# Attention rows of tiles 10 to 31 transposed by 32x32 blocks and DMA, with a new order of instructions

## Chip, cores, metric

One Trainium2 chip, one of its cores. The metric is the device time of one execution in microseconds (us); the kernel before is given as the median of three runs.

## The reference

Two blocks, applied twice in turn to one sequence of 2048 rows of 512 (bf16): attention with a sliding window of 256 and 32 heads of 16, and an MLP with 1792 hidden units.

```python
def _A_ref(x, wqkv, wo):
    B, S, D = x.shape
    H = 32; Dh = D // H; W = 256
    qkv = (x @ wqkv).reshape(B, S, 3, H, Dh)  ...
    scores = jnp.einsum("bhqd,bhkd->bhqk", q, k) * (Dh ** -0.5)
    mask = (idx[:, None] - idx[None, :] >= 0) & (idx[:, None] - idx[None, :] < W)
    p = _softmax(jnp.where(mask[None, None], scores, -1e9), axis=-1)
    o = jnp.einsum("bhqk,bhkd->bhqd", p, v)
    return o.transpose(0, 2, 1, 3).reshape(B, S, D) @ wo

def _B_ref(x, w1, b1, w2, b2):
    return jnp.einsum("bsf,fd->bsd", _gelu(x @ w1 + b1), w2) + b2

x = A_x
for _ in range(2):
    x = x + _A_ref(_layernorm(x), A_wqkv, A_wo)
    x = x + _B_ref(_layernorm(x), B_w1, B_b1, B_w2, B_b2)
```

## The kernel before

The rows are cut into 16 tiles of 128, and because the two blocks are applied twice the kernel counts tiles (tau) from 0 to 31; tile tau works on the rows of tau modulo 16. Attention goes by blocks of two tiles, b = 0 to 15. X holds all rows in SBUF and is updated in place.

For each tile and each of the two layers (0 is attention, 1 is the MLP) `layernorm` takes the statistics on VectorE (DVE), a power on GpSimd (POOL), and writes the normalised rows, xn, on DVE. The projections need these rows transposed. This is done in one of two ways:

- On TensorE (PE): four 128x128 transposes into a PSUM bank (the function `tr`, line 36 of the profile, since a helper records every PE operation as line 32 or 36), then a copy out by DVE (line 916) or ScalarE (ACT, line 918).
- By blocks and DMA, where `by_dma` says so; in the kernel before for the MLP rows of tiles 4 to 29. DVE transposes each 32x32 block in place of its own (line 952) into xs_, four DMAs write it to a scratch array scr_x in DRAM in pieces of 256 bytes (line 956), and one DMA reads it back into xnTB in pieces of 1024 bytes (line 960). All DMAs are issued by SP, in order, and xs_ has three buffers.

xnTB, the MLP's input, keeps the four 32-row groups of a tile outside the four feature chunks, so a partition's row is one piece of 1024 bytes. xnTA, the input of the Q, K and V projections, has the chunk outside and the 256 rows of a block contiguous, as both operands of PE read it. xnTA has two halves, so block b+2 can be written only when PE has finished Q, K and V of block b. The V projections of a block are late in PE's order, the Q projections of the next are the first to need the new contents.

Attention of a block: groups of scores (32x64 tiles of PE, 64 to 320 columns) into pairs of PSUM banks, exponentials on ScalarE (line 1111), mask products on DVE or POOL (line 1132), the product with V on PE into a pair of banks, a stream transpose of the result on DVE (line 1197), reciprocal and product (1200, 1202), a transpose back (1207), the output projection and the residual (990). An MLP job takes two or four tiles: W1 matmuls, Gelu on ScalarE (1269, 1278), W2 matmuls, residual.

Nothing is scheduled on the chip. `_Plan` holds a node for each piece of work, with its engine, a planned duration, what it reads and writes, and for PE the class of PSUM banks it needs. ORDER, a list of node numbers written out in the file, sets the order on every engine; a negative number takes a node's alternative engine. `_Plan.follow` walks it and gives each PSUM request the candidate in its pool that comes free first. `_Sched` turns the nodes into instructions with semaphore waits. SP's DMAs take turns on 12 semaphores, and a DMA waits for the one that had the semaphore before it.

Of the kernel before, what the change touches and what calls it, by code (L numbers as in the profile page):

```python
# [6 lines left out]
dt = mybir.dt  # L7
# [511 lines left out]
def bass_interleave_layers__sliding_block__dense_activation_gelu__prompt_kernel(  # L519
# [42 lines left out]
    NXS = 3  # L562
    NSC = 16

    def by_dma(tau, layer):
        return layer and 4 <= tau < NT - 2
# [23 lines left out]
    def mm(n):  # L590
        return n / 2.4 + 2.6

    with ExitStack() as kctx:
        S_ = _Sched(nc, kctx)

        def sb(name, shape, dtype=dt.bfloat16):
# [21 lines left out]
        scr = nc.dram_tensor("scr_x", (NSC, 4, 32, 4, P), dt.bfloat16, kind="Internal").ap()  # L618
# [17 lines left out]
            0, 18, 1, 19, 2, 20, 8, 4, 5, 21, 6, 14, 7, 22, 15, 16, 9, 23, 33, 10, 24, 11, 40, 12, 34, 3, 41, 17, 35,  # L636
            42, 84, 36, 43, 85, 86, 37, 44, 38, 77, 87, 45, -40, 88, -47, 78, 89, 79, 80, 47, 57, 58, 81, 59, 60, 90,
            82, 61, 52, -84, 48, 49, 50, 91, -52, 92, 229, 25, 93, 94, 53, 26, 108, -96, 54, 55, 96, 109, -57, 101,
            154, 62, 155, 63, 102, 230, 64, 103, 236, 65, 72, 156, 67, 110, 66, 68, 111, 69, 70, -72, 145, 112, 73,
            231, 104, 146, 358, 74, 75, 232, 97, 98, 359, 76, 147, 99, 135, 136, 237, 105, 158, 28, -101, 815, 137, 27,  # L640
            160, 138, 360, 106, 139, 361, 113, 29, 140, 141, 159, 13, 30, 107, 142, 143, 365, -149, 149, -145, 114,
            125, 366, 126, 587, -163, 115, 31, 127, 32, 128, 594, 151, 150, 116, 117, 118, 588, 233, 163, -120, 595,
            129, -162, 120, 165, 121, 122, 253, 123, 951, -154, 254, 164, 183, 367, 958, 255, 256, 184, 368, 238, 124,
            -153, 257, 185, 187, 130, 131, 239, 240, 188, 132, 816, 234, 133, 596, 189, 235, 597, 178, 134, 241, -167,
            180, 263, 258, 259, 242, 264, 179, 369, 192, 362, 265, 959, 193, 266, 960, 589, 191, 243, 248, 167, 249,
            194, 244, 182, 245, 190, 246, 250, 822, 251, -268, 168, 157, -253, 186, 268, 169, 260, 961, 247, 261, -196,
            262, 170, 172, 173, -197, 174, 286, 269, 287, 270, -182, 271, 363, 817, 175, 288, 364, 273, 171, 370, 272,
            274, -177, 197, 371, 198, 275, 291, 199, 293, -277, 372, 373, 200, 292, 177, 277, 374, 823, 375, 279, 290,
            378, 376, 379, -202, 278, 377, 282, 295, 283, 384, 281, 385, 380, 202, -295, 381, 284, 311, 382, 386, 387,
            313, 289, 216, 217, 388, 218, -281, 203, -384, 219, 204, 312, 205, 220, 206, -286, 315, 207, 316, 208, 300,  # L650
            317, 209, 296, 210, 221, 211, 301, 298, 222, 212, 223, 302, 297, 224, 320, 322, 225, 213, 214, 226, -300,
            321, 227, 404, 430, 405, -320, 431, 416, 432, 417, 420, 406, 418, 421, 306, 323, 325, 413, 307, 414, 422,
            -319, 427, 415, 423, 428, 308, 424, 429, 408, 824, 425, 459, 410, 464, 310, 465, 444, 469, 309, 466, 467,
            460, 598, 409, 445, 446, 470, 303, 389, 314, 390, 391, 304, 392, 326, 590, 305, 215, 439, 447, 468, 393,
            440, 441, 442, 433, 449, 327, 443, 952, 419, 450, 328, 451, 434, 426, 471, 452, 472, 454, 461, 453, 462,
            455, 435, 473, 436, 591, 437, 456, 448, 457, 329, 518, 438, 411, 399, 463, -331, 400, 458, 401, 402, 592,
            403, 489, 394, 228, 395, 331, 396, 397, 520, 490, 398, 491, 492, 493, 593, 519, 494, 412, 504, 332, -408,
            505, 333, 334, 335, 495, 336, 506, 496, 508, 497, 337, 498, 510, -508, 345, 346, 338, 347, 348, 509, 513,
            349, -522, 499, 500, 515, 501, 502, 474, -512, 503, 475, 514, 476, 533, 1216, 599, 825, 535, 477, 600, 478,
            479, 339, 516, 480, 534, 481, 350, 340, 528, 482, 517, 530, 483, 512, 484, 485, 351, 486, 352, 341, 529,  # L660
            487, 953, 353, 342, 488, 537, 354, 539, 522, 343, -533, 1209, 355, 538, 523, 356, 357, 542, 524, 671, 543,
            672, -532, 657, 658, 673, 544, 640, 525, 324, 664, 1210, 665, 641, 1211, 659, 668, -546, 669, 666, 654,
            655, 642, 670, 644, 656, -537, 661, 662, 646, 601, 663, 602, 603, 541, 604, 645, 606, 540, 635, 1217, 546,
            607, 636, 526, 608, 547, 527, -649, 637, 609, 548, 610, -606, -640, 649, 549, 611, 650, 616, 617, -644,
            618, 619, 651, 550, 612, 620, 631, 818, 613, 632, 614, -552, 705, 675, 676, 615, 706, 677, 707, 708, 690,
            678, 685, 344, 686, 691, 680, 552, 692, 687, 681, 688, 693, 660, 682, 683, 570, 652, 571, 694, 647, 572,
            689, 573, 653, 553, 667, 826, 554, 555, 819, 709, 556, 574, 710, 674, 711, 712, 713, 695, 696, 557, 679,
            697, 698, 700, 684, 701, 702, 575, 703, 621, 699, 622, 714, 558, 623, 624, 704, 626, 627, 559, 625, 628,
            629, 715, 576, 630, 716, 717, 820, 633, 577, 764, 821, 718, 560, 766, 827, 561, 719, 828, 720, 578, 721,
            765, 829, 634, 830, 831, 638, 755, 579, 749, 757, 580, 962, 750, 756, 832, -834, 759, 770, 751, 722, 771,  # L670
            723, 724, 725, 726, 772, 562, 745, 563, 834, 747, 835, 773, 567, 836, 1218, 774, 837, 565, 727, 746, 838,
            728, 583, 760, 566, 729, 730, 762, 581, 731, 748, 732, 564, 733, 758, 734, 761, 769, 863, 752, 735, 736,
            865, 763, 737, 738, 767, 739, 1345, 568, 864, 775, 584, 753, 582, 776, 754, -868, 877, 777, 849, 878, 850,
            740, 741, 742, 879, 778, 743, 868, -780, 744, 851, 869, 852, 839, 853, 840, -882, 841, 870, 842, 780, 859,
            844, 843, 860, 845, -872, 846, 847, 861, 848, 901, -769, 854, 855, 902, 856, 862, 857, 781, 954, 858, 782,
            903, 872, 955, 783, 1219, 784, 874, 798, 785, 799, -867, 800, 801, 873, 786, 892, 956, 802, 894, 963, -876,
            975, 957, 976, 787, 977, 964, 893, 978, 788, 803, 897, 789, 965, 899, 966, 804, 876, 880, 898, 805, 790,
            882, 806, 791, 967, 884, 886, 807, 794, 808, 814, 792, 883, 968, 795, 887, 1346, 979, 810, -970, 793, 811,
            905, 1004, 812, 888, 970, 1006, 809, 585, 1005, 1352, 796, 995, 896, 980, 981, 997, 885, 982, 983, 900,
            813, 996, -905, 906, 971, 984, 972, 908, 973, 1212, -896, 907, 974, 1008, 1043, 1009, 909, 1044, 910, 1045,  # L680
            1010, 911, 889, 999, -891, 1046, 1000, 1047, 1050, -1013, 891, 1001, 1060, 1347, 1048, 1061, -999, 912,
            1062, -1004, 1033, 913, 985, 1034, 1051, 569, 986, 987, 1052, 1035, 988, 1018, 989, 990, 1020, 991, 914,
            992, 993, 915, 1053, 1019, 994, 1013, 1054, 1014, 916, -1022, 1233, 1234, 1055, 1235, 1015, 1236, 1028,
            1007, 917, 1237, 1030, 918, 919, 920, 1074, 934, 1029, 921, 1075, 1076, 1077, 1017, 1038, 1213, 1057, 1032,
            1039, 1353, 1058, 1031, 1011, 935, 1040, 1089, 1016, 1090, 1064, 1354, 1002, 1065, 922, 1066, 1022, 1059,
            1067, 923, 1049, 1023, 1094, 1024, 1068, 1095, 1079, 1080, 1078, 1081, 1082, 924, 1091, 1083, 1092, 925,
            1069, 1099, 1093, 926, 1100, 1101, 1355, 1070, 1063, 1071, -1037, 1096, 936, 937, 1056, 586, 1072, 938,
            1102, 1097, 1084, 1103, 1085, 939, 933, 1086, 1087, 1073, 1266, 940, 941, 927, 1104, 1098, 797, 1105, 1106,
            1088, 1107, 929, 1108, 1109, 928, 1110, 942, 1111, 1112, 943, 1113, 1114, 944, 1149, -1042, 1267, 1214,
            1150, 1215, 1151, 947, 1152, 1025, 1268, 1115, 945, 1026, 1253, 948, 1153, 1255, 1220, 1154, 930, 1155,  # L690
            1037, 946, 1116, 1117, 1254, 1156, 1118, 1257, 1157, 1258, 1158, 1590, 1159, 1160, 1027, 1161, 949, 1162,
# [176 lines left out]
        for h in range(NZ):  # L868
            PL.root = (add("pe", clear, 8 * mm(512), reads=["zero", "g0"], writes=["ps:init0", "ps:init1"], prio=-200, geo="f"),)
# [489 lines left out]
```

## Time and profile before

| | |
|---|---|
| median of three runs | 462.32 us (461.71 to 462.74) |
| profiled execution: its time, its span | 461.4 us, 459.7 us |
| PE busy | 442.2 us, 96%, 8793 matmuls |
| DVE busy | 370.0 us, 81% |
| ACT busy | 394.2 us, 86% |
| POOL busy | 216.5 us, 47% |
| PE transposes | 152 (38 tiles), of these 128 for attention |
| granted TensorE clock | 1.00 |
| DMA, all queues | 27855 packets, 18.17 MB |
| scr_x writes | 104, 32 KB each, 1.6 us to landing |
| xnTB reads | 26, 128 KB each, 2.1 us to landing |

An engine's busy share is over the whole span; the busy tenths show it in 40 slices. The chain of waits follows the work that ended last back to its releaser at every step, so it tells which engine sets the time in each stretch. Idle time in front of a group is given with what ended it. PE's busy time is modelled where matmuls overlap.

### The profile page before, as it was taken

How to read it: one execution, taken by the hardware profiler on the slowest of the kernel's cores; microseconds unless marked ns; L12 is line 12 of the kernel's file. 1: busy time of each engine (PE TensorE's matmuls, PEld its weight loads, DVE VectorE, ACT ScalarE, POOL GpSimd, SP SyncE). 2: the span in 40 equal slices, each digit the busy share in tenths (PEclk: the TensorE clock that was granted, in tenths of full speed). 3: DMA queues.
4: the chain of work that ended last, by engine and by line, in shares of the span. 5: the costliest groups of instructions: out<-in, count | busy, mean ns of one | idle time of the engine just before them, and what ended most of it. 6: DMA issues, size and time to landing. Idle time of an engine off the chain costs nothing.

```text
span 459.7 us, 19399 instructions
## 1 busy us (share of the span) xinstructions
PE 442.2 (96%) x8793; PEld 236.5 (51%) x8793; DVE 370.0 (81%) x754; ACT 394.2 (86%) x473; POOL 216.5 (47%) x250
## 2 busy tenths in 40 slices
PE   6987899999889999999999999999999999999997
PEld 3654465754444445555435545546454554454663
DVE  5999878989989688995879988988888968896312
ACT  2999999999989989899996999979997999875442
POOL 4466636712653555553667654462344415451600
PEclk9999999999999999999999999999999999999999
DMA  7670000001020110100030110101030021102011
GB/s 228 206 266 3 4 3 3 5 1 37 8 55 3 20 31 15 37 3 9 16 74 5 27 23 12 40 4 19 3 66 26 6 57 31 43 5 70 13 58 47
DMA packets 27855, 18.17 MB, mean 40 GB/s; under 512 B 15868, under 2 KB 27260, under 8 KB 27772
## 3 DMA queue, kind: packets, MB, share of 16 engines
q1 hardware_dynamic: 27772, 16.92, 13.8%
q8 instruction: 69, 1.13, 1.0%
q14 instruction: 14, 0.11, 0.1%
HBM read 11.41 MB, written 5.51 MB: 37 GB/s over the span
## 4 chain that ended last, share of the span: by engine, by line
PE 70%; ACT 23%; DVE 2%; SPq 1%; DMA 1%; POOL 1%; issue 1%; DVEq 0%; POOLq 0%
PE ps L32 69%; ACT E L1111 18%; ACT gT L1278 2%; PE ps L36 1%; SPq L956 1%; ACT gT L1269 1%; ACT L1111 1%; DMA scr_x<-xs_ 1%; ACT Va L918 1%; ACT QT L918 1%; DVE KT L1030 1%; DVE gT L1266 0%; DMA xnTB<-scr_x 0%; SPq L960 0%; DVE xs_ L952 0%
## 5 line engine op out<-in xcount | busy, mean ns | idle before, releaser
L1111 ACT ACTIVATE E<-ps 128x1024 bf16<-128x1024 f32 x304 | 287.0, 1046 | 26.9 <-PE ps L32 26.3
L1132 POOL TENSOR_TENSOR E<-E,mask 128x512 bf16<-128x512 bf16 (+1 forms) x120 | 125.5, 1059 | 121.6 <-DVE E L1132 43.3
L32 PE MATMUL ps<-W_sb,gT 128*128 128x512 bf16 x448 | 118.3, 380 | 0.0
L32 PE MATMUL ps<-xnTB,W_sb 128*128 128x512 bf16 (+1 forms) x560 | 116.0, 337 | 0.9 <-DMA xnTB<-scr_x 0.7
L990 DVE TENSOR_TENSOR X<-X,ps 128x512 bf16<-128x512 bf16 x64 | 43.5, 683 | 40.3 <-PE ps L32 39.3
L32 PEld LDWEIGHTS ps<-xnTB,W_sb 128*128 128x128 bf16 x560 | 51.2, 98 | 46.0 <-ACT E L1111 2.9
L32 PE MATMUL ps<-QT,KT 32*64 32x320 bf16 (+4 forms) x2976 | 65.4, 258 | 6.6 <-ACT E L1111 4.8
L32 PE MATMUL ps<-xnTA,Wqkv_sb 128*128 128x256 bf16 x512 | 70.1, 274 | 0.7 <-ACT E L1111 0.4
L1278 ACT ACTIVATE gT<-ps,b1T 128x512 bf16<-128x512 f32 (+1 forms) x92 | 48.8, 588 | 22.1 <-PE ps L32 21.6
L940 POOL TENSOR_TENSOR rstd<-veps,mhalf 128x1 f32<-128x1 f32 x64 | 36.5, 575 | 57.0 <-DVE veps L937 55.7
L32 PEld LDWEIGHTS ps<-W_sb,gT 128*128 128x128 bf16 x448 | 39.5, 98 | 42.7 <-issue 5.9
L1132 DVE TENSOR_TENSOR E<-E,mask 128x512 bf16<-128x512 bf16 (+1 forms) x142 | 57.5, 433 | 4.6 <-ACT E L1111 4.5
L32 PEld LDWEIGHTS ps<-xnTA,Wqkv_sb 128*128 128x128 bf16 x512 | 46.0, 98 | 19.3 <-issue 2.9
L32 PEld LDWEIGHTS ps<-QT,KT 32*64 32x64 bf16 x2976 | 27.6, 103 | 51.6 <-ACT E L1111 35.6
L32 PE MATMUL ps<-E,Va 64*17 64x128 bf16 (+3 forms) x3872 | 49.0, 229 | 2.0 <-ACT E L1111 0.7
L1197 DVE STREAM_TRANSPOSE TT<-ps 128x1024 f32<-128x1024 f32 x32 | 39.9, 1245 | 11.6 <-PE ps L32 11.0
L32 PEld LDWEIGHTS ps<-E,Va 64*17 64x17 bf16 x3872 | 39.3, 85 | 19.0 <-PE ps L32 5.4
L1241 POOL TENSOR_TENSOR X<-X,b2b 128x512 bf16<-128x512 bf16 x32 | 36.7, 1157 | 17.9 <-DVE xn L943 6.4
L933 DVE BATCH_NORM_STATS2 stat<-X 128x6 f32<-128x512 bf16 x64 | 43.4, 683 | 1.4 <-DMA X<-in_A_x_dram 0.7
L1030 DVE TENSOR_TENSOR KT<-ps,parmask 128x1024 bf16<-128x1024 f32 x32 | 38.4, 1211 | 3.9 <-PE ps L32 3.7
L1266 DVE TENSOR_SCALAR gT<-ps,b1T 128x512 bf16<-128x512 f32 (+1 forms) x48 | 31.8, 672 | 5.7 <-PE ps L32 5.3
L32 PE MATMUL ps<-Wqkv_sb,xnTA 128*128 128x512 bf16 x128 | 35.2, 381 | 0.2 <-ACT E L1111 0.2
(49 smaller groups left out, 325.2 us busy)
## 6 DMA issues: line engine op xcount, KB each, us to landing
W_sb<-in_B_w_dram SPq DMA_DIRECT2D x2, 1792.0 KB, 12.9
scr_x<-xs_ SPq DMA_DIRECT2D x104, 32.0 KB, 1.6
xnTB<-scr_x SPq DMA_DIRECT2D x26, 128.0 KB, 2.1
out_dram<-X SPq DMA_DIRECT2D x16, 128.0 KB, 1.8
Wqkv_sb<-in_A_wqkv_dram SPq DMA_DIRECT2D x3, 512.0 KB, 6.4
X<-in_A_x_dram SPq DMA_DIRECT2D x3, 512.0 KB, 4.8
X<-in_A_x_dram SPq DMA_DIRECT2D x2, 256.0 KB, 2.9
Wo_sb<-in_A_wo_dram SPq DMA_DIRECT2D x1, 512.0 KB, 6.4
```

Of the source, the lines that this page charges most:

```text
L32: return self.e.matmul(*a, **k)
L918: alt=() if kind not in ACT_OK and not boot else (("act", lambda e, B: e.activation(dst(B), src(B), AF.Copy, scale=1.0), d_act(n) + 14, 0. ...
L933: add("dve", lambda e, B: e.bn_stats(stat6[:, k6, :], X[:, t, :]), 590, reads=["X%d" % t], writes=["st%d" % k6], prio=prio)
L940: add("pool", lambda e, B: e.tensor_tensor(out=rstd[:, k : k + 1], in0=veps[:, k : k + 1], in1=mhalf[:], op=ALU.pow), 535, reads=["ve%d" % ...
L990: add("dve", lambda e, B: e.tensor_tensor(out=X[:, t, :], in0=X[:, t, :], in1=ps[:, B[g][0], :], op=ALU.add), d_psum(512), reads=["X%d" % ...
L1030: add("dve", lambda e, B, g=g, i=i: e.tensor_tensor(out=KT[:, kb, :, 2 * i : 2 * i + 2, :].rearrange("p a c q -> p a (c q)"), in0=ps[:, B[ ...
L1111: add("act", lambda e, B, g_=g_, gi=gi: e.activation(E[:, 2 * gi : 2 * gi + 2, e0 : e0 + 512], ps[:, B[g_][0] : B[g_][0] + 2, :], AF.Exp, ...
L1132: op = lambda e, B, Ew=Ew, Mw=Mw: e.tensor_tensor(out=Ew, in0=Ew, in1=Mw, op=ALU.mult)
L1197: add("dve", lambda e, B: e.transpose(TT[:, s].rearrange("p a c q d -> p (a c q d)"), ps[:, B[g][0] : B[g][0] + 2, :].rearrange("p a n -> ...
L1241: add("pool", lambda e, B: e.tensor_tensor(out=X[:, t, :], in0=X[:, t, :], in1=b2b[:], op=ALU.add), 1110, reads=["X%d" % t, "b2b"], writes ...
L1266: add("dve", lambda e, B, g=g, fc=fc: e.tensor_scalar(out=gT[:, fc, 0:M], in0=ps[:, B[g][0], 0:M], scalar1=b1T[:, fc : fc + 1], scalar2=No ...
L1278: add("act", lambda e, B, g=g, fc=fc: e.activation(gT[:, fc, 0:M], ps[:, B[g][0], 0:M], AF.Gelu_apprx_tanh, bias=b1T[:, fc : fc + 1], scal ...
```

## The change

Attention rows of tiles 10 to 31 are transposed by DVE and DMA too. As xnTA keeps its layout, the read back is four DMAs, one for each feature chunk, and the source comes in pieces of 32 elements, 64 bytes: 512 pieces in each. Their stream transposes use one buffer of xs_ of their own (the fourth, xs3), and their scratch is separate. The banks of scores and of the product with V may be pairs that begin at an odd bank. The list ORDER is new for all nodes (3449, 3295 before). The planned duration of the first bank clears is changed, not what they do.

```diff
-    NXS = 3
+    NXS = 4
...
     def by_dma(tau, layer):
-        return layer and 4 <= tau < NT - 2
+        return 4 <= tau < NT - 2 if layer else tau >= 10
...
-        scr = nc.dram_tensor("scr_x", (NSC, 4, 32, 4, P), dt.bfloat16, kind="Internal").ap()
+        scr = nc.dram_tensor("scr_x", (2 * NSC, 4, 32, 4, P), dt.bfloat16, kind="Internal").ap()
...
-            0, 18, 1, 19, 2, 20, 8, 4, 5, 21, 6, 14, 7, 22, 15, 16, 9, 23, 33, 10, 24, 11, 40, 12, 34, 3, 41, 17, 35,
+            3, 15, 18, 4, 16, 5, 19, 6, 8, 20, 9, 10, 21, 0, 22, 1, 2, 23, 40, 24, 11, 12, 33, 14, 17, 41, 34, 42, 35,
...
-            "sc": [(0, 1, 2, 3), (4, 5, 0, 1), (2, 3, 4, 5), (6, 7, 0, 1), (2, 3, 6, 7), (4, 5, 6, 7)],
+            "sc": [(0, 1, 2, 3), (4, 5, 0, 1), (2, 3, 4, 5), (6, 7, 0, 1), (2, 3, 6, 7), (4, 5, 6, 7)] + [
+                (a, a + 1, c, c + 1) for a in range(7) for c in range(a + 2, 7) if a % 2 or c % 2],
             "o": [(6,), (7,), (5,), (4,), (3,), (2,), (1,), (0,)],
-            "od": [(6, 7), (4, 5), (2, 3), (0, 1)],
+            "od": [(6, 7), (4, 5), (2, 3), (0, 1), (5, 6), (3, 4), (1, 2)],
...
-            PL.root = (add("pe", clear, 8 * mm(512), reads=["zero", "g0"], writes=["ps:init0", "ps:init1"], prio=-200, geo="f"),)
+            PL.root = (add("pe", clear, (16 - 6 * h) * mm(512), reads=["zero", "g0"], writes=["ps:init0", "ps:init1"], prio=-200, geo="f"),)
...
-                z = xs_rr[0] % NXS
-                v = xs_rr[0] % NSC
-                xs_rr[0] += 1
+                z = xs_rr[1] % (NXS - 1) if layer else NXS - 1
+                v = xs_rr[layer] % NSC + (0 if layer else NSC)
+                xs_rr[layer] += 1
...
-                dma(lambda e, B: e.dma_start(dst.rearrange("p r d j -> p (r d j)"), scr[v].rearrange("q i r c -> (q i) (r c)")),
-                    quads(dname), reads=["scr%d_%d" % (v, r) for r in range(4)], prio=prio, dur=2800.0, issue=400.0)
+                if layer:
+                    dma(lambda e, B: e.dma_start(dst.rearrange("p r d j -> p (r d j)"), scr[v].rearrange("q i r c -> (q i) (r c)")),
+                        quads(dname), reads=["scr%d_%d" % (v, r) for r in range(4)], prio=prio, dur=2800.0, issue=400.0)
+                    return
+                for d in range(DC):
+                    dma(lambda e, B, d=d: e.dma_start(
+                        dst[:, :, d, :], scr[v].rearrange("q i r (d j) -> (q i) r d j", d=DC)[:, :, d, :]),
+                        [quads(dname)[d]], reads=["scr%d_%d" % (v, r) for r in range(4)], prio=prio, dur=5000.0, issue=400.0)
                 return
```

On PE's order as the list sets it, 16 of 38 groups of four transposes are left, and the changes between full-array work, scores and products with V number 362, 379 before. SP's order has 192 scr_x writes (104 before), 88 reads into xnTA (none before) and the same 26 reads into xnTB.

## The prediction

> **What bounds the kernel now.** I read the page's busy lines first, then the chain of waits in order of time, then the windows cut where the chain changes hands, then groups, DMA and SP.
>
> The busy tenths, 11.5 us a slice:
>
> ```profile
> PE   6987899999889999999999999999999999999997
> DVE  5999878989989688995879988988888968896312
> ACT  2999999999989989899996999979997999875442
> ```
>
> The chain of waits in order of time (start us, us, what), early and late:
>
> ```profile
> 23.75 9.16 ACT E L1111 x10
> ...
> 111.95 12.97 ACT E L1111 x14
> ...
> 138.06 20.50 PE ps L32 x313
> ...
> 205.85 0.22 PE ps L36 x4
> ...
> 289.20 28.73 PE ps L32 x460
> ```
>
> Two stages with two limits. Until about 140 us the chain lives on ScalarE's exponentials; after it, it is TensorE almost unbroken, and a group of four transposes stands in it with 0.22 us. I cut at the 112th of the 304 exponentials (the 56th score group), which starts at 141.3 us. The columns are us, then busy us (count) by engine:
>
> ```profile
> 0.00:141.30 141.30, 128.06 (x2847) 73.14 (x2847) 122.22 (x270) 127.30 (x155) 73.59 (x94) 1.00 0.22 67
> 141.30:300.00 158.70, 157.61 (x3217) 80.63 (x3216) 136.23 (x281) 146.87 (x168) 85.04 (x92) 1.00 0.11 23
> ```
>
> Ahead of the cut PE is free 13.2 us, and ScalarE only 14.0, mostly the start before the first exponential. Behind it PE is free 1.1 us of 158.7 with the granted clock at 1.00: a us taken off PE there is a us off the end, if nothing new makes PE wait. So the change has to be costed by stage.
>
> **The change, part by part.** 22 groups of four PE transposes go, each with its evacuation. Rows of groups (us, mean ns of one):
>
> ```profile
> L36 PE MATMUL ps<-ident,xn 128*128 128x128 bf16 x152 | 14.3, 220 | 1.2 <-ACT E L1111 0.7 <-ACT xnTA L918 0.6
> L916 DVE COPY xnTA<-ps 128x512 bf16<-128x512 bf16 x25 | 10.3, 414 | 2.4 <-PE ps L36 2.1
> L952 DVE STREAM_TRANSPOSE xs_<-xn 128x512 bf16<-128x512 bf16 x26 | 18.3, 705 | 1.3 <-DMA scr_x<-xs_ 0.8
> ```
>
> *PE, late stage.* The 220 ns of one transpose overlap; what a group occupies is the chain's 0.22 us. In before, tiles 10 to 15 are transposed ahead of the cut and 16 to 31 behind it (158 to 338 us); in the new order 16 of the 22 removed groups also lie behind the 112th exponential. 16 x 0.22 = 3.5 us. The new order also changes between full-array, score and PV matmuls 362 times, not 379; behind the cut 238, not 249. A change costs what this PE timeline shows (start, us):
>
> ```profile
> 215.10 1.25 PE L32 MATMUL ps<-W_sb,gT 128*128 128x512 bf16 x5
> 216.19 0.81 PE L32 MATMUL ps<-Wo_sb,OT 128*128 128x512 bf16 x3
> 216.93 0.43 PE L32 MATMUL ps<-QT,KT 32*64 32x64 bf16 x24
> ```
>
> Five matmuls take 1.09 us from start to start, 0.217 each. The next three take 0.74 before a score group starts, 0.09 more than 3 x 0.217. So 11 x 0.09 = 1.0 us. Against it three V matmuls move behind the cut and one MLP matmul ahead: +0.4. Late stage: -3.5 - 1.0 + 0.4 = -4.1 us.
>
> *Early stage.* PE loses 6 groups (1.3 us), 6 changes (0.5) and the moved matmuls (0.4): 2.3 us. ScalarE has the same work there: one Q and one V evacuation fewer, two normalised tiles more, all near 0.6 us. DVE gains 8 stream transposes (8 x 0.705 = 5.6) and loses 8 copies (3.3) and six mask products net (2.5, five at 0.44 and one small; they go to GpSimd, half idle there); one Q, one V and one OT more (2.1) and the rest of three normalisations (1.0) make it +2.9 on 122.2. So -2.3 if PE set the end, +2.9 if DVE did. The nearest row is ScalarE's: the chain's long pieces are its exponentials and their number is the same. I take 0 and keep both ends.
>
> *DVE, late stage.* 14 stream transposes (9.9) for 12 copies (5.0) and two xnTB copies more (0.8): +5.7 on some 248 us in 318. Hidden behind PE; if that cover failed it would be all of it.
>
> *SP.* Per tile four writes, at the 432 ns that is the median issue of the 104 there are now, and four reads. A read has 512 pieces, as each Wqkv load has, which took 469 to 507 ns to issue. 88 x 0.43 + 88 x 0.5 = 82 us more on a queue that now issues for 54 and waits most of the rest:
>
> ```profile
> SPq L956 <- DVE xs_ L952: 208.5, 10, 86.7
> ```
>
> Enough room on the whole. What counts is the order on it: the reads wait until PE has read the other contents of that half of xnTA, and behind a waiting read stand scratch writes of the next tile and of MLP tiles; for those wait the single buffer xs3 (DVE, and all masks behind it) and the MLP's first matmuls. In before PE waited 0.66 us for an MLP read at 239.7 us, so such a path can surface.
>
> *The reads.* No read in 64-byte pieces is in the trace. Two windows price packets, 105 to 112 us (mostly 256-byte writes) and 422.2 to 425.4 (mostly 1024-byte):
>
> ```profile
> DMA packets 935, 0.30 MB, mean 43 GB/s; under 512 B 867, under 2 KB 933, under 8 KB 933
> ...
> q1 hardware_dynamic: 933, 0.26, 22.4%
> ```
>
> ```profile
> DMA packets 432, 0.39 MB, mean 123 GB/s; under 512 B 48, under 2 KB 432, under 8 KB 432
> ...
> q1 hardware_dynamic: 432, 0.39, 40.1%
> ```
>
> The second: 0.401 x 16 x 3.2 us = 20.5 us; less 48 small ones, 19.3 us for 384: 50 ns. The first: 0.224 x 16 x 7 = 25.1 us, less 66 at 50 ns: 21.8 us for 867, 25 ns. The line through both meets 64 bytes at 19 ns. Upper bound 25 (the smaller piece no dearer than the 256-byte one) for the sum, and the rival below goes past it; I take 19. A read puts 32 pieces on each of 16 engines: 0.62 us. The 128-piece read lands 2.1 us after issue with 8 x 50 ns = 0.4 in it, so 1.7 is latency. The eight reads of a block: 8 x 0.62 + 1.7 = 6.7 us from release to the last landing (8.1 at 25 ns). PE's cover is the work that its new order has between the last V matmul on a half and the first Q matmul of the block two on. Adding it up by the spacing of the timeline: 6.2 us for block 7, 7.5 for 14, 8.2 for 6, 11.8 or more for 5, 8 to 13 and 15. Exposed: 0.5 us at 19 ns, 1.9 + 0.6 = 2.5 at 25. I take 0.5.
>
> [...]
>
> *Bank pairs, the fourth xs buffer, more scratch.* No instruction of their own; they act through the order, already counted.
>
> **Sum.** -4.1 + 0 + 0.5 = -3.6 us: span 459.7 to 456.1. That execution took 461.4 with 1.7 around the span; the median of the three runs is 462.32, so the forecast is 462.32 - 3.6 = 458.7.
>
> **Rivals.** *Dear pieces (slower).* Each piece costs well over the 256-byte packet, reads queue on the 16 engines, and PE waits at the first Q matmul of a block. At 40 ns: 8 x 32 x 40 ns + 1.7 = 11.9 us; beyond the cover by 5.7 (block 7), 3.7 (6), 4.4 (14), 0.1 (13): 13.9 us. 462.3 - 4.1 + 13.9 = 472.1. It decides from about 28 ns, where the overruns (2.7, 0.7, 1.4) make up for the gain. For it: 28 is near 25. Against: in this trace the packet's time falls with its size. [...]
>
> *DVE in order.* DVE sets the early stage (+2.9), being 122 of 141 us busy there, and a stream transpose waiting for xs3 holds the masks: 0.07 + 4 x 0.43 + 1.6 = 3.4 us from one to the next, where DVE's order has 3.1 us of work at its second and third. 462.3 - 4.1 + 0.5 + 2.9 + 0.3 = 461.9, no change. Against it: DVE's idle time before L952 is 1.3 us over 26 now.
>
> *Larger gain.* PE's early 2.3 us count too, between 100 and 140 us, where chain pieces alternate between PE and ScalarE: 462.3 - 4.1 - 2.3 = 455.9.
>
> *Not done.* It is: 16 groups of transposes stay in PE's order of 38.
>
> **How the numbers follow.** Forecast 0.60, dear pieces 0.15, DVE 0.15, larger gain 0.10. Its own range is 455.9 to 461. The range to hold 8 in 10 starts at 454.7 (larger gain, plus the 1.1 us that PE idles from 141 to 300) and ends at 464.0 (-4.1 + 2.5 + 2.9 gives 463.6; a little of the dear pieces). Within 0.2%, 0.9 us, is what a measurement here can't tell from no change. Faster: nearly all of 0.60, 0.10, and a little of DVE: 0.70. Same: most of DVE: 0.09. Slower: dear pieces and the rest: 0.21.
>
> **What would show it.** Right: transposes 64 in PE's row, PE busy near 100% in every window behind the cut, reads of xnTA landing under 4 us, the 112th exponential within 2 us of 141.3. Wrong: PE waiting on DMA xnTA at blocks 6, 7 or 14 for over 4 us together, DVE xs_ waiting on DMA scr_x by several us, or the cut moved past 144 us.

## The result, and the profile after

The kernel after takes 488.94 us (median of 4 runs, 486.29 to 491.68); the kernel before, measured beside it, 462.03. The ratio is 1.058 (95% interval 1.052 to 1.064): slower by 27 us, where 3.6 us less was forecast, and outside the range. The profiled execution has a span of 484.5 us; the forecast for it was 456.1.

The page of the kernel after: busy time, the 40 slices (12.1 us each), the DMA packets and the chain by engine.

```profile
PE 446.9 (92%) x8705; PEld 235.3 (49%) x8705; DVE 376.2 (78%) x758; ACT 392.1 (81%) x467; POOL 220.0 (45%) x252
PE   8988999969799999798989979899989999989997
PEclk9999999998889999899999998999999999999999
DMA packets 86991, 23.94 MB, mean 49 GB/s; under 512 B 75004, under 2 KB 86396, under 8 KB 86908
PE 57%; ACT 19%; DVE 9%; SPq 7%; DMA 5%; issue 2%; POOL 1%; DVEq 0%
```

The slices of PE that were 9 in a row now have 6, 7 and 8 among them, and the granted clock is an 8 in five. In the chain of waits VectorE, SP's queue and DMA hold 21% of the span, 4% before.

The windows, cut at the 112th exponential (us, then busy us and count by engine, clock, DMA share):

```profile
0.00:146.80 146.80, 129.91 (x2821) 73.78 (x2822) 125.64 (x270) 127.80 (x154) 81.54 (x102) 0.97 0.32 77
146.80:484.50 337.70, 317.02 (x5886) 161.51 (x5883) 250.59 (x489) 264.26 (x314) 138.48 (x151) 0.98 0.21 37
```

The early stage is 5.5 us longer than before (141.3), the late one 19.3 (459.7 - 141.3 = 318.4 before). Where do they go? First the waits of SP and of the other engines (engine, line, releaser: us in total, times, longest):

```profile
SPq L965 <- DVE xs_ L961: 66.0, 16, 12.5
SPq L974 <- PE ps L32: 43.6, 9, 8.9
```

```profile
ACT E L1126 <- PE ps L32: 46.9, 40, 7.1
DVE X L1005 <- PE ps L32: 32.9, 22, 14.0
DVE xs_ L961 <- DMA scr_x<-xs_: 13.3, 6, 4.0
PE ps L32 <- DMA xnTB<-scr_x: 3.7, 2, 3.5
PE ps L32 <- DMA xnTA<-scr_x: 2.5, 3, 1.7
```

L974 is the line of the new reads, L965 of the scratch writes. SP stands 43.6 us in front of reads because PE has not yet released that half of xnTA. A stream transpose stands 13.3 us in front of its buffer, six times. PE itself waits only 2.5 us for the reads. ScalarE waits for PE's scores 46.9 us, 26.3 before. The chain in order of time (start us, us, what) shows how one follows from the other:

```profile
93.95 2.10 PE ps L32 x33
...
96.07 0.52 SPq L974
...
96.63 0.63 SPq L974
...
97.31 0.63 SPq L974
...
97.98 1.72 SPq L974
...
100.42 0.63 SPq L974
...
101.09 3.62 DMA scr_x<-xs_
...
104.74 1.31 DVE xs_ L961 x2
...
107.09 0.98 DVE E L1147 x3
108.06 0.61 DVE X L1005
...
108.72 1.38 PE ps L32 x9
```

Three of a tile's four writes out of xs3 had been issued by 94.3 us; SP's order puts six of a block's eight reads ahead of the fourth. At 96.05 PE has done its last matmul on that half of xnTA, and the six reads are issued one after the other, one of them in 1.72 us. The fourth write goes out at 101.09 and has landed at 104.72. Only then is xs3 free. VectorE does nothing from 101.3 to 104.7, and behind the waiting stream transpose stand mask products (L1147) and a residual (L1005); PE waits for the residual. From PE's release to the work that hung on it are 12.7 us; PE has other work for most of them and stands idle for the last 3.4, from 105.4 us on.

What PE loses while it waits it can lose a second time. Windows around a PE wait for an MLP read:

```profile
194.50:198.10 3.60, 0.11 (x17) 0.00 (x0) 0.23 (x2) 1.94 (x2) 3.60 (x6) 1.00 0.38 95
198.10:201.50 3.40, 3.37 (x9) 1.27 (x10) 0.79 (x2) 0.00 (x0) 0.06 (x1) 0.56 0.13 20
```

PE works 0.11 of 3.6 us, and for the next 3.4 us the granted clock is near a half (0.56): 9 matmuls start where 16 would at 0.217 us each. Over the span the clock is 0.979, that is 0.021 x 484.5 = 10.2 us of full-speed time. The idle time need not be that long, nor is its length all that counts: in this trace 2.0 us without work (from 250.9) are also followed by 3.4 us at half clock (0.50 from 253.09 to 256.50), and in that of the third experiment below the 2.7 us that PE waits for an MLP read are not (1.00 from 145 us on).

The new reads themselves (duration ns of an issue, min/median/max; then us to landing):

```profile
L974 SPq DMA_DIRECT2D xnTA<-scr_x x88: 517/628/1898, 65.8 to 363.1; - x88
...
DMA to landing us min/median/max: 2.0/2.5/4.0
```

The trace's DMA records give the 45,056 pieces of 64 bytes 11 ns each (median); the 256-byte packets, nearly all of them writes to the scratch, take 25. A piece costs less than the 19 ns of the forecast, the issue of a read more than its 0.5 us.

### The profile page after: what moved, and what is told of

It reads as the page before. It is cut to its first block, busy times and chain, and to the rows that moved or that the text cites. A ratio compares the mean times of both kernels' runs of the same rounds, so it can differ in the third digit from the quotient of the medians.

```text
span 484.5 us, 19471 instructions
## 1 busy us (share of the span) xinstructions
PE 446.9 (92%) x8705; PEld 235.3 (49%) x8705; DVE 376.2 (78%) x758; ACT 392.1 (81%) x467; POOL 220.0 (45%) x252
## 3 DMA queue, kind: packets, MB, share of 16 engines
q8 instruction: 68, 1.11, 1.0%
## 4 chain that ended last, share of the span: by engine, by line
PE 57%; ACT 19%; DVE 9%; SPq 7%; DMA 5%; issue 2%; POOL 1%; DVEq 0%
PE ps L32 57%; ACT E L1126 14%; SPq L974 4%; DMA scr_x<-xs_ 3%; SPq L965 3%; ACT gT L1293 2%; DVE stat L942 2%; DVE xs_ L961 1%; DVE X L1005 1%; DVE E L1147 1%; DVE KT L1045 1%; ACT gT L1284 1%; ACT L1126 1%; DMA xnTA<-scr_x 1%; DMA xnTB<-scr_x 1%
## 5 line engine op out<-in xcount | busy, mean ns | idle before, releaser
L1126 ACT ACTIVATE E<-ps 128x1024 bf16<-128x1024 f32 x304 | 286.7, 1044 | 47.7 <-PE ps L32 46.9
L1147 POOL TENSOR_TENSOR E<-E,mask 128x512 bf16<-128x512 bf16 (+1 forms) x122 | 127.9, 1063 | 119.3 <-DVE E L1147 59.0
L32 PE MATMUL ps<-xnTA,Wqkv_sb 128*128 128x256 bf16 x512 | 73.3, 283 | 12.0 <-DVE X L1005 6.3
L32 PE MATMUL ps<-QT,KT 32*64 32x320 bf16 (+4 forms) x2976 | 66.9, 262 | 8.0 <-ACT E L1126 3.4
L1005 DVE TENSOR_TENSOR X<-X,ps 128x512 bf16<-128x512 bf16 x64 | 43.4, 681 | 33.8 <-PE ps L32 32.9
L32 PEld LDWEIGHTS ps<-xnTA,Wqkv_sb 128*128 128x128 bf16 x512 | 48.1, 101 | 35.0 <-DVE X L1005 7.0
L1147 DVE TENSOR_TENSOR E<-E,mask 128x512 bf16<-128x512 bf16 (+1 forms) x140 | 53.3, 408 | 5.2 <-ACT E L1126 4.7
L32 PE MATMUL ps<-E,Va 64*17 64x128 bf16 (+3 forms) x3872 | 50.4, 234 | 4.2 <-POOL E L1147 2.2
L32 PEld LDWEIGHTS ps<-E,Va 64*17 64x17 bf16 x3872 | 40.3, 86 | 21.6 <-PE ps L32 7.4
L961 DVE STREAM_TRANSPOSE xs_<-xn 128x512 bf16<-128x512 bf16 x48 | 33.6, 702 | 14.4 <-DMA scr_x<-xs_ 13.3
```

The lines of the kernel that those rows point to most:

```text
L32: return self.e.matmul(*a, **k)
L961: add("dve", lambda e, B: e.transpose(xs_[:, z, :].rearrange("p (q d j) -> p d q j", q=4, d=DC), xn[:, s, :].rearrange("p (d q j) -> p d q ...
L1005: add("dve", lambda e, B: e.tensor_tensor(out=X[:, t, :], in0=X[:, t, :], in1=ps[:, B[g][0], :], op=ALU.add), d_psum(512), reads=["X%d" % ...
L1126: add("act", lambda e, B, g_=g_, gi=gi: e.activation(E[:, 2 * gi : 2 * gi + 2, e0 : e0 + 512], ps[:, B[g_][0] : B[g_][0] + 2, :], AF.Exp, ...
L1147: op = lambda e, B, Ew=Ew, Mw=Mw: e.tensor_tensor(out=Ew, in0=Ew, in1=Mw, op=ALU.mult)
```

## The experiments

The theory after the result: SP's order makes the loss. Reads that wait for PE, and that take 0.63 us each to issue (the median), stand ahead of scratch writes that are ready; the single buffer xs3 carries the delay to VectorE, and from there to PE. The rivals: the one buffer is enough of a cause; the pieces, or the number of them, are; or the new order of the computing engines is bad in itself. In all runs but the four replanned ones the place of every PSUM request in the banks is written out as the kernel after has it, so that moving a node on SP moves no bank. Ratios are against the kernel before, run on the same chip; 1% is 4.6 us.

### A second buffer for the attention rows

```diff
-    NXS = 4
+    NXS = 5
...
-                z = xs_rr[1] % (NXS - 1) if layer else NXS - 1
+                z = xs_rr[1] % 3 if layer else 3 + xs_rr[0] % 2
```

To make room the raw bias is loaded into gT and the statistics tiles are indexed modulo 32.

> The attention rows take two buffers of xs in turn, not one; order and banks as in the changed kernel. Theory A (SP: eight reads at 0.63 us to issue, and scratch writes stand behind reads that wait for PE): the wait of DVE for scr_x falls from 13.3 us to under 4, but the reads and the MLP's writes are as late as before; time 478 to 485 us, a third of the loss of 27 us back or less. Theory B (the single buffer xs3 holds DVE, all else follows from it): DVE's wait gone and 462 to 470 us. Theory C (the transfer of 64-byte pieces): no change, 486 to 491. Theory D (the new order with its bank pairs is bad by itself): no change.

Measured: 478.13 us, ratio 1.031 (1.028 to 1.035), span 475.6. The stream transpose waits for the scratch write once, 4.3 us. Of the 5.8% the second buffer gives back 2.7, which is more than the third that theory A allowed: the single buffer carries about half of the loss, and the rest goes past it. The reads and writes of the MLP rows stand in the same queue, and PE waits 5.2 us for xnTB here; that the whole rest goes that way is not shown.

### The same number of reads in 256-byte pieces

```diff
                     dma(lambda e, B, d=d: e.dma_start(
-                        dst[:, :, d, :], scr[v].rearrange("q i r (d j) -> (q i) r d j", d=DC)[:, :, d, :]),
+                        dst[:, :, d, :], scr[v].rearrange("q i r (s j) -> (q i) r s j", s=DC)[:, d, :, :]),
```

Each read takes the four chunks of one row group instead of one chunk of four, so that blocks stand in other places of xnTA, and the kernel leaves out putting them right; bytes, DMAs, order and waits are the same.

> Each read into xnTA takes one contiguous piece of 256 bytes per partition (128 pieces, not 512); the feature blocks so land in the wrong places, which this leaves out. Same number of DMAs, same order, same banks, same waits. Theory A: a read's issue falls from 0.63 us to 0.34 to 0.45, SP has 16 to 25 us more, and the kernel comes to 455 to 464 us. Theory B: SP is quicker behind a release, so something comes back, but the buffer stays: 472 to 482. Theory C: the pieces are 11 ns each already and a read lands in 2.5 us; if the transfer were the cause the landing falls to about 2.0 and the time with it, at an unchanged issue time. Theory D: 484 to 491.

Measured: 471.66 us, ratio 1.017 (1.012 to 1.022), span 469.9. The reads:

```profile
L993 SPq DMA_DIRECT2D xnTA<-scr_x x88: 319/432/1653, 66.8 to 344.2; - x88
...
DMA to landing us min/median/max: 1.6/1.9/3.7
```

With 128 pieces instead of 512 an issue takes 0.43 us, not 0.63, and 4.1 of the 5.8% come back. The transfer got cheaper too: a read lands 0.6 us sooner, 0.4 of it behind its issue, and a 256-byte piece of a read takes 18 ns where the four 64-byte pieces for it took 44. So the number of pieces was on the path, by SP's issue time (88 x 0.2 = 17 us less), by the landing, or by both: this run, which changes both, can't part theories A and C.

### SP's order alone

Each tile's four writes are put directly behind their stream transpose in the list; the nodes of all other engines keep their order. In words, since the list holds only numbers:

```diff
-  three writes of a tile, six reads of an earlier block, fourth write, two reads, ...
+  four writes of a tile, eight reads of an earlier block, ...
```

> SP's order alone is changed: every tile's four scratch writes stand directly behind their stream transpose in the list, so that no read that waits for PE is ahead of a write that is ready. Reads, pieces and all other engines' orders as in the changed kernel, banks fixed. Theory A: DVE's wait for scr_x falls to under 4 us, PE's waits behind it go, 464 to 475 us; what stays is the issue time of the reads. Theory B: the same or better, as the buffer comes free early. Theory C and D: 484 to 491.

Measured: 466.94 us, ratio 1.006 (1.003 to 1.009), span 464.1, granted clock 0.996. SP's waits, the other engines' and the chain by engine:

```profile
SPq L1002 <- DVE xs_ L998: 73.2, 21, 14.6
...
SPq L1011 <- PE ps L32: 23.5, 9, 8.0
```

```profile
DVE xs_ L998 <- DMA scr_x<-xs_: 0.9, 2, 0.7
```

```profile
PE 63%; ACT 28%; DMA 3%; DVE 2%; SPq 2%; issue 2%
```

Nothing was taken out, nothing made cheaper, and 5.2 of the 5.8% are back, with SP's wait for PE at 23.5 us instead of 43.6 and xs_ at 0.9 instead of 13.3. This settles the cause of those 5.2%: it is SP's order.

### Another layout of xnTA: one read per tile

```diff
-        xnTA = sb("xnTA", [P, 2, DC, 2 * P])
+        xnTA = sb("xnTA", [P, 2, 2 * P, DC])
...
-                pe_group(g, [(Wqkv_sb[:, dc, which * D + kc * P : which * D + (kc + 1) * P], xnTA[:, xs, dc, :],
+                pe_group(g, [(Wqkv_sb[:, dc, which * D + kc * P : which * D + (kc + 1) * P], xnTA[:, xs, :, dc],
```

One DMA with 1024-byte pieces takes the place of four; both operands of PE are read with a step of 8 bytes.

> xnTA keeps the four feature chunks innermost (a token's four chunks side by side), the stream transpose writes its blocks with that stride, and a tile is read back by one DMA of 1024-byte pieces instead of four of 64-byte pieces. Q, K and V read xnTA with a stride of 8 bytes. Order as in the changed kernel less three of four reads, banks fixed. Theory A: 66 DMAs fewer on SP, about 44 us less issue, time 452 to 460 us if PE and DVE take the stride at no cost; if the strided operands cost, Q, K and V matmuls (640) or the stream transposes (0.70 us) are longer and say by how much. Theory B: 465 to 480. Theory C: as A. Theory D: 484 or more.

Measured: 520.07 us, ratio 1.121 (1.118 to 1.124). The group by shapes:

```profile
L32 PE MATMUL ps<-xnTA,Wqkv_sb 128*128 128x256 bf16 x512 | 129.3, 403 | 2.6 <-DVE gT L1310 1.1 <-DVE X L1034 0.7 <-ACT xnTA L960 0.7
```

283 ns of one becomes 403, 512 times: PE is 56 us longer for it. The stream transposes that write the strided layout take 985 ns (702), the copies out of PSUM 1298 (414). The V projections, where xnTA is the stationary operand, stay at 386 (381). The cheap read is bought at far too high a price, and the layout with 64-byte pieces is the better of the two.

### Order and cheap reads together

Writes first, as in the third experiment, and 256-byte pieces, as in the second, again without putting the blocks right.

> Writes directly behind their transposes (as e3) and reads of one contiguous 256-byte piece per partition (as e2; the feature blocks land in the wrong places, which this leaves out). It says what a read's issue time is still worth once no write stands behind a waiting read. Theory A (SP: issue time and order): the eight reads of a block go out in 3.8 us, not 5.4; e3's 467 us come to 458 to 463. Theory B (the single buffer): e3 has already freed the buffer, so within 1 us of e3. Theory D (new order and bank pairs): within 1 us of e3.

Measured: 462.86 us, ratio 0.998 (0.996 to 1.000), span 460.9, granted clock 1.000. All of the loss is gone, yet the forecast gain is not there. The 112th exponential starts at 141.6 us, 0.3 later than before. From it to the 192nd the kernel takes 110.2 us, 2.1 less than before; from there to the 272nd 111.7, 2.0 more; and behind that 97.4, 1.1 more. These are single traces, and executions of the kernel before lay between 461.9 and 465.9 us on this chip. The chain in the middle one of the three:

```profile
335.19 1.41 issue
336.59 4.24 PE ps L32 x51
...
344.05 1.22 DVE KT L1082
...
348.90 1.25 DVE TT L1249
...
354.31 1.20 DVE X L1042 x2
```

In the kernel before, TensorE held 98% of the chain from 305 to 409 us. Here a stretch of 12 us goes for the most part through VectorE, but little time is lost in it: PE is busy for 11.5 of these 12.3 us, and from the 192nd to the 272nd exponential it waits for VectorE about half a us in all. The longest wait there is the 1.41 us of "issue", a wait that ends on nothing the profile shows. PE's total can't be read from this trace, which lacks 72 of its 8705 matmul records. The third experiment's has them all, and the order of the computing engines is the same. Its waits over the whole span:

```profile
PE ps L32 <- issue: 5.1, 6, 1.6
...
PE ps L32 <- DMA xnTB<-scr_x: 2.7, 1, 2.7
...
PE ps L32 <- DVE Va L962: 0.5, 2, 0.3
```

Behind the cut they are 3.7, 2.7 and 0.5 us, 6.9 together, where PE in the kernel before has 1.2 and none on "issue". PE's busy time behind the cut is 311.8 us there, 314.1 before. So 2.3 us of PE's work went, and 5.7 us of new waits came. In the trace of this experiment the wait for the MLP read is 0.8 us; the "issue" waits stay. The last section says of them what the traces show.

### Order and second buffer together

> Writes directly behind their transposes (as e3) and two buffers of xs for the attention rows (as e1). Theory A: DVE waited 0.9 us for scr_x in e3, so the second buffer has nothing left to free; 465 to 468 us, within 1.5 us of e3. Theory B: the buffer is a cause of its own and e6 is 3 us or more under e3.

Measured: 466.74 us, ratio 1.006 (1.004 to 1.009), the same as with the order alone. Once the writes are not held up, the single buffer costs nothing.

### Another order on SP alone

As in the third experiment only SP's nodes move, now by a search over their places with measured issue times.

> The changed kernel with another order on SP alone, PE, DVE, ACT and POOL and the banks exactly as in it. It asks how much of the loss of 27 us was SP's order by itself. Theory A: better than e3's 467 us, 458 to 464. Theory D: no better than e3; 466 or more.

Measured: 465.59 us, ratio 1.007 (1.005 to 1.009), span 463.7: not better than the simple rule, and 1.6 us above what was expected. Of two orders on SP neither brings the gain; that none could is not shown.

### All engines replanned, with and without the DMA path

If the new order itself is what eats the gain, an order planned with the measured issue times should bring it. Two such lists were made for the kernel after, and as controls two for the kernel before, by the same search with the same durations: one pair with 0.76 us for a read and 0.56 for a write, the other with 0.69 and 0.49, the slow issues and the half clock.

> The changed kernel's work, DMAs and pieces, with a new list ORDER made with the issue times that the trace shows (0.76 us for a read, 0.56 for a write, queue gaps and slow issues in it) in place of 0.40; banks fixed. Theory A: the path is sound and its loss was the planned issue time; PE loses 16 groups of transposes behind the cut, so 453 to 459 us, 1 to 2% under before. Theory D: an order as tight as this loses whatever the DMAs cost; 463 us or more.

> Control: the kernel before (all attention rows transposed by PE), its list ORDER made anew in the same way with the same issue times; banks fixed. If what e7 gains is only a better search, this gains the same. Theory A: PE has the 4.9 us of transposes and stays the bound; 457 to 462 us, and e7 is 3 to 6 us under it.

> The changed kernel's work, DMAs and banks with a new list ORDER, made with 0.69 us for the issue of a read and 0.49 for a write, and with 1.0 us more for an issue that meets a fetch of PE's instructions (26 of the 27 issues over 0.9 us in the changed kernel's trace overlap a 16 KB packet of the instruction queue; of 273 that overlap none not one is over 0.8), and with PE at half clock after a long wait. Theory A (issue time and order on SP, the slow issues in it): 450 to 458 us, 1 to 3% under before. Theory D (an order with less PE work is tighter and loses it in waits whatever SP costs): 463 or more.

> Control: the kernel before with a list ORDER made anew in the same way, slow issues and half clock in it, banks as before. What e9 gains over this is the DMA path's own; what this gains over before is the search. Theory A: 456 to 461 us, 4 to 6 above e9. Theory D: this one is faster than e9.

| | us | ratio |
|---|---|---|
| after, replanned | 469.03 | 1.013 (1.009 to 1.017) |
| before, replanned | 468.01 | 1.009 (1.006 to 1.013) |
| after, replanned, slow issues | 468.61 | 1.012 (1.010 to 1.015) |
| before, replanned, slow issues | 468.68 | 1.012 (1.010 to 1.015) |

All four came out slower than theory A said. The 463 us or more that theory D gave for the two of the kernel after did come, but the controls lost as much: the search finds worse orders than the list of the kernel before. So they say nothing about a best order for the DMA path. What they do say comes from the pairs: with the same search the path makes a difference of +1.0 and -0.1 us, within the intervals none, in place of -3.6.

No version beat the kernel before by more than can be measured.

## Why the prediction was wrong

- **The step that failed:** "SP ... 82 us more ... Enough room on the whole. What counts is the order on it", and then a price of nothing for that order. The order was what counted: with SP's order alone put right, 24 of the 27 us go (5.81% - 0.61% = 5.2%). Two things were mis-sized with it. A read was priced at 0.5 us from the Wqkv loads; it takes 0.63, and some issues 1 to 2 us. SP's issues come to 181 us against 76 before (the 54 of the prediction is the scratch writes alone), 105 more instead of 82: the reads 60, not 44, the writes 42 more, not 38, and the xnTB reads 2. The slow issues were there to see: the 104 writes of before take 432 ns in the median but 517 in the mean. And the time that SP waits for PE with ready writes behind it, 43.6 us, had no term in the sum.
- **The rival "DVE in order"** named the mechanism, a stream transpose that waits for xs3 and holds the masks, but priced it at 0.3 us. It reckoned 3.4 us from one stream transpose to the next, which holds for four writes issued one behind the other. In the chain shown above, the last write left SP five microseconds of reads later. A latency that runs through an in-order queue has to be worked out from what stands ahead in that queue.
- **"Dear pieces"** is refuted: 11 ns a piece, not 19, let alone the 40 of its sum, which no run shows. In place of the forecast's 0.5 us for exposed reads PE waited 2.5, and landing is 2.5 us in the median, 4.0 the longest, against the 4 that were named.
- **Early stage 0:** right once SP is out of the way (141.4 and 141.6 us at the cut in the third and fifth experiment, 141.3 before); VectorE's +2.9 measured +3.4 and didn't set the end.
- **Late stage -4.1:** the work left PE's order as counted (64 transposes of 152 are left). But only 2.3 us of busy time went with it (third experiment, 311.8 against 314.1), and PE's own waits, which the sum had at 0.5 us for the reads alone, grew by 5.7. So, as far as one trace tells, the work was saved in part and the gain went into waits of PE: one for an MLP read (2.7 us, 0.8 in the fifth experiment) and the "issue" waits (3.7). VectorE's +5.7 behind the cut measured +2.8, and with SP's order put right "hidden behind PE" held but for 0.5 us.
- **The range** starts 0.1 us too low: 455.9 less 1.1 is 454.8. Nothing hangs on it.
- **What would show it wrong** was named rightly: xs_ waiting for scr_x by several us (13.3), the cut past 144 us (146.8).

The half clock added to the loss, by up to 10.2 of the 27 us; in the fifth experiment, where nothing is lost, the clock is 1.000. It was in no term: in the trace of before PE's longest wait behind the first matmuls is 1.0 us and the clock is 1.000 over the whole span.

## What to carry to other kernels

A queue that issues in order has to be priced like an engine, by what stands in front of each entry and what that entry waits for, not by its total. A transfer that must wait for a late consumer belongs behind every transfer that is ready, above all if a single buffer hangs on it: here SP's order was worth 24 of the 27 us. And where an edit takes work off the bounding engine, that engine's new waits have to be added up beside the work saved: here 5.7 us of waits stood against 2.3 us of work, with SP's order already put right.

## What was not expected of the hardware

SP's slow issues fall together with instruction fetches. The page of the kernel after has a queue of 68 packets of 16 KB, 1.11 MB, which is 64 bytes for each of PE's 17,410 matmuls and weight loads; the first comes when PE has started 225 of these, the last when it has started 17,267, one for every 254. So they are taken to be PE's instructions:

```profile
q8 instruction: 68, 1.11, 1.0%
```

Leaving out the input loads at the start, 26 of the 49 DMA issues of SP that overlap such a packet take over 0.9 us; of the 273 that overlap none, not one does (0.79 at most, median 0.43). In the kernel before it is 11 of 21 against none of 125. What these slow issues take beyond 0.55 us each adds up to 22 us of SP's time in the kernel after and 11 in the one before. The window of the 1.72 us issue shown in the chain:

```profile
DMA packets 1057, 0.08 MB, mean 43 GB/s; under 512 B 1056, under 2 KB 1056, under 8 KB 1056
...
q8 instruction: 1, 0.02, 3.8%
```

The one packet that is not a small one is the fetch. Among the input loads that are left out, one of the kernel after takes 0.94 us with no fetch beside it; why was not tried.

PE's longer "issue" waits go with the fetches too. In the trace of the kernel after, from 20 us on, PE stands idle five times for over 0.7 us (0.8 to 1.8) without anything in the profile that ends it, and each time the idle stretch ends 1.4 to 1.5 us behind the end of a fetch packet. For the longest the packet lies at 356.55 to 357.68 us; PE is idle from 357.39 and goes on at 359.17. Four of the five begin behind 5,057, 13,505, 14,529 and 16,321 of PE's records, numbers that differ by multiples of 256, which at 64 bytes each is one packet; the one from 219.5 us on does not fit. So in those four PE seems to have waited for its own instructions. For the 1.41 us of the fifth experiment shown above the packet lies at 333.99 to 335.31 us, and PE goes on at 336.59. The kernel before has 69 such packets and no such wait; what makes the difference was not tried.

The other: SP took 0.43 us to issue a read of 128 pieces and 0.63 for one of 512, with the bytes the same, though the number alone does not set it (a Wqkv load, of 512 pieces of 1024 bytes, takes 0.46 to 0.51), while on the DMA engines a 64-byte piece took 11 ns and a 256-byte one of a read 18.
